# Single-row loads, small fp32 matmuls to spread them, row centring on GpSimd, and a new order of steps, in a linear-attention kernel with a feed-forward layer

## The chip, the cores and the metric

The kernel runs on one core of a Trainium2 chip. A core has five engines, each with its own in-order instruction stream: TensorE (PE; its weight loads are shown apart as PEld), VectorE (DVE), ScalarE (ACT), GpSimd (POOL) and SyncE (SP, which here only issues DMAs). Matmuls write to PSUM, the other operands lie in SBUF. Sixteen DMA engines move data between the memories; a DMA is issued from the queue of an engine, here mostly SyncE's. The metric is the device time of one execution in microseconds (us), lower is better.

## What is computed

A linear attention with decay (RWKV-like) over 4 batches, 8 heads, 768 steps and head size 48, then a layer norm, a feed-forward layer of 384 to 1536 to 384 with a ReLU, and a residual. Inputs and output are fp32.

```python
# r, k, v: (4, 8, 768, 48); w, u: (8, 48)
for t in range(S):
    kt, vt, rt = (k[:, :, t].copy(), v[:, :, t].copy(), r[:, :, t].copy())
    cur = np.einsum('bhd,bhe->bhde', u[None] * kt, vt)
    y[:, :, t] = np.einsum('bhd,bhde->bhe', rt, state + cur)
    state = w[None, :, :, None] * state + np.einsum('bhd,bhe->bhde', kt, vt)
...
# x: y with the heads side by side, (4, 768, 384)
mu = np.mean(x, axis=-1, keepdims=True)
var = np.mean((x - mu) ** 2, axis=-1, keepdims=True)
xn = (x - mu) / np.sqrt(var + 1e-06) * g_ln
ch = np.maximum(xn @ w_ch1, 0.0) @ w_ch2
return (x + ch).astype(np.float32)
```

## The kernel before

The sequence of each batch is cut into 6 chunks of 128 steps, 24 chunks in all. Inside a chunk the recurrence is written as matrix products: k is scaled by w to the power −(t+1) and r by w to the power t (the tables Fk and Fr), their product under a causal mask gives the scores, and a state Z carries what earlier chunks left. The tables come from log w: one copy of w spread over all 128 partitions (WB, L178), its logarithm (LN, L232), and two exponentials whose scale is a column of step numbers (FR at L238, FK at L235). The same w, and u, are also needed as columns, with the head dimension along the partitions: four small loads (ROWS, L186) bring them as 48 × 4 columns of two partition halves. From them come uwI (UW, the product u·w) and WLZ (WL, the power 128 of w, by which the state decays over a chunk). The scale g of the layer norm is spread over the partitions by a load (GB, L181).

For each chunk i the steps are, in the names of the code: LK, LR, LV load k, r, v (128 partitions × 8 heads × 48, 192 KB each, all from SyncE's queue); SK and SR scale k and r into the bf16 tile sc (L168, the helper `times`, on VectorE or GpSimd); CV casts v to vv; TR turns sc by eight TensorE transposes (L284), TC copies them out of PSUM to trs; for chunks from 9 on a transposing DMA (TD, L305) does it instead. AT makes the scores (L320), AM masks them (L330, VectorE), Q multiplies r and k columns (L168). S gives the diagonal term and the new state (L351, L364), CC copies the diagonal's factors, ZU and ZD form the state Z, VB multiplies v by the diagonal's factors (L383), Y sums up the output in PSUM (L393, L401), X adds the diagonal and row sums (L408, VectorE). Then SQ takes the squares on ScalarE, RS the reciprocal root on GpSimd, and XN centres the row and multiplies by g (L421 the mean, L422 one VectorE operation); the reciprocal root is applied only at the very end, since the ReLU lets a positive factor through. LT and XT (or the transposing DMA LTD) turn xn; UP is the up-projection (L458), RL the ReLU out of PSUM into hT (ScalarE L474 or VectorE L476), DN the down-projection (L486), OT scales and adds x (L542), STO stores. Chunks 8 to 19 go through the up-projection in pairs, the others alone (GROUPS). The last chunk's down-projection is done in two halves (DA, DB, L501; OA, OB, L517) so that the first can be stored while the second runs. Weights w1 and w2 come as three loads each from GpSimd's queue, cast to bf16 on the way (IW1, IW2).

TensorE has work only once chunks have been loaded, scaled and turned; until then steps named DU run matmuls on a tile of zeros (L227, L229), their size in columns written in the plan.

The order is written out by hand: PLAN is one list of steps, each with its number and the engine (v VectorE, s ScalarE, g GpSimd, − fixed). Every engine executes its share of the list in the list's order, and waits by semaphores for what its operands need; tiles rotate through small rings (SLOTS), and the PSUM tiles named tr, at, s, y and o exist once each.

## Time and profile before

| | us |
|---|---|
| median of 3 runs | 162.78 |
| lowest and highest run | 160.44, 163.22 |
| the profiled execution | 160.98 |
| its span, first to last instruction | 159.2 |

| engine | busy us | share of the span | instructions |
|---|---|---|---|
| TensorE matmuls | 143.0 | 90% | 1769 |
| VectorE | 132.3 | 83% | 265 |
| GpSimd | 88.3 | 55% | 119 |
| ScalarE | 69.4 | 44% | 155 |

The granted TensorE clock is 1.00 throughout. The queue of SyncE carries 98,560 packets, 23.8 MB, most of them of 192 bytes (one head's row of one step).

The page has, besides totals, the busy share of each engine in 40 equal slices; a view by stretch gives the same in microseconds between chosen times. The chain of waits follows the work that ended last back to what released it; "SPq L186" in it means that SyncE's queue was issuing the DMA of line 186, "DMA kf<-in_k_dram" that a load of k was in flight. A line of the timeline has the start, the duration, the engine, the line, the operation, output and inputs and, in brackets, how long the engine stood idle before and what released it. Durations of the helper lines (L163, L165, L168) belong to several steps, so they are told apart by their tiles.

### The profile page before, as it was taken

Reading aid. Unit: us, or ns where it says so; the run is one execution under the profiler, and the core shown is the slowest. Engines: PE = TensorE matmul, PEld = TensorE weight load, DVE = VectorE, ACT = ScalarE, POOL = GpSimd, SP = SyncE. Lnnn points to the kernel's source line nnn. Section 1 sums busy time; section 2 is a strip of 40 time slices with the busy share of each in tenths; the row PEclk is TensorE's granted clock in tenths of the full one; section 3 lists DMA queues with packets and bytes.
Section 4 is the critical chain, followed back from the end, with each engine's and each line's share of the span. In section 5 each row is a group of like instructions: output and inputs, shape, how many; then the busy total and the mean of one; then the engine's idle time right before and its main releaser. Section 6 shows DMA issues by size and latency. Waiting matters only on the chain.

```text
span 159.2 us, 4407 instructions
## 1 busy us (share of the span) xinstructions
PE 143.0 (90%) x1769; PEld 109.1 (69%) x1769; DVE 132.3 (83%) x265; ACT 69.4 (44%) x155; POOL 88.3 (55%) x119
## 2 busy tenths in 40 slices
PE   5896959499999989799999988997999999999991
PEld 2244737398877777677787757784787767888881
DVE  2457998696899999998889999999979999996132
ACT  3427644653821844646653644614184412700510
POOL 2332465899594665979769865559327420850100
PEclk9999999999999999999999999999999999999999
DMA  3899999999989959999999999895899772314212
GB/s 89 156 173 211 184 184 191 216 199 232 198 157 182 192 110 215 168 218 122 247 235 183 219 224 145 207 214 105 180 215 197 157 195 45 124 29 124 99 54 101
DMA packets 100356, 26.64 MB, mean 167 GB/s; under 512 B 95344, under 2 KB 99952, under 8 KB 100336
## 3 DMA queue, kind: packets, MB, share of 16 engines
q1 hardware_dynamic: 98560, 23.80, 75.0%
q0 software_dynamic: 1632, 2.36, 8.9%
q8 instruction: 14, 0.23, 0.6%
q10 hardware_dynamic: 144, 0.20, 0.5%
q14 instruction: 6, 0.05, 0.1%
HBM read 19.27 MB, written 4.72 MB: 151 GB/s over the span
## 4 chain that ended last, share of the span: by engine, by line
DVE 37%; PE 29%; SPq 10%; POOL 8%; issue 8%; DMA 6%; ACT 0%; DVEq 0%; POOLq 0%
PE hp L458 13%; PE o L486 12%; DVE A L330 8%; DVE xn L422 6%; DVE x L408 4%; SPq L265 4%; DVE Z L168 3%; DMA kf<-in_k_dram 3%; DVE ot L542 3%; DVE hT L476 3%; DVE ZS L377 3%; POOL sc L168 3%; DVE sc L168 3%; DMA trs<-sc 2%; SPq L262 2%
## 5 line engine op out<-in xcount | busy, mean ns | idle before, releaser
L458 PE MATMUL hp<-xT,w_sb 128*128 128x128 bf16 (+1 forms) x648 | 57.6, 238 | 0.6 <-DVE hT L476 0.6
L486 PE MATMUL o<-w_sb,hT 128*128 128x384 bf16 x276 | 53.3, 326 | 2.9 <-DVE ot L542 2.9
L458 PEld LDWEIGHTS <-w_sb 128*128 128x128 bf16 x648 | 48.7, 114 | 5.2 <-issue 0.7
L474 ACT ACTIVATE hT<-hp 128x512 bf16<-128x512 f32 x51 | 30.2, 596 | 44.9 <-PE hp L458 44.3
L486 PEld LDWEIGHTS <-hT 128*128 128x128 bf16 x276 | 25.2, 97 | 15.5 <-issue 3.4
L330 DVE TENSOR_TENSOR A<-at,mask 128x1024 bf16<-128x1024 f32 x24 | 29.1, 1215 | 1.8 <-PE at L320 1.8
L383 POOL TENSOR_TENSOR Vb<-vf,cc 128x384 f32<-128x384 f32 x14 | 12.3, 876 | 13.7 <-DVE cc L165 7.0
L422 DVE SCALAR_TENSOR_TENSOR xn<-x,mu,g_bc 128x384 bf16<-128x384 f32 x24 | 19.0, 792 | 0.8
L168 POOL TENSOR_TENSOR sc<-rf,Fr 128x384 bf16<-128x384 f32 x14 | 15.6, 1117 | 7.2 <-DMA rf<-in_r_dram 7.2
L542 DVE SCALAR_TENSOR_TENSOR ot<-o,rs,x 128x384 f32<-128x384 f32 x23 | 14.0, 610 | 5.8 <-PE o L486 5.7
L168 POOL TENSOR_TENSOR q<-trs 128x512 bf16<-128x512 bf16 x13 | 16.3, 1251 | 2.3 <-ACT trs L163 2.2
L428 POOL TENSOR_SCALAR rs<-sq 128x1 f32<-128x1 f32 (+1 forms) x18 | 3.9, 217 | 23.5 <-ACT sqj L415 22.5
L168 POOL TENSOR_TENSOR sc<-kf,Fk 128x384 bf16<-128x384 f32 x12 | 13.4, 1119 | 5.8 <-DMA kf<-in_k_dram 5.8
L476 DVE TENSOR_SCALAR hT<-hp 128x512 bf16<-128x512 f32 x21 | 14.3, 683 | 2.6 <-PE hp L458 2.6
L408 DVE SCALAR_TENSOR_TENSOR x<-y,Vb 128x384 f32<-128x384 f32 x24 | 13.2, 550 | 2.8 <-POOL Vb L383 2.1
L415 ACT ACTIVATE sqj<-x,sm 128x384 bf16<-128x384 f32 x24 | 14.7, 613 | 1.8 <-DVE cc L165 1.1
L227 PE MATMUL o<-warm 128*128 128x512 bf16 x45 | 13.3, 433 | 1.7 <-DVE u_p L194 1.7
L163 ACT COPY trs<-tr 128x1024 bf16<-128x1024 bf16 x8 | 8.1, 1011 | 12.5 <-PE tr L284 12.5
L168 DVE TENSOR_TENSOR sc<-kf,Fk 128x384 bf16<-128x384 f32 x12 | 9.0, 750 | 5.0 <-ACT Fk L235 4.5
L431 POOL TENSOR_TENSOR rs<-rs,expo 128x1 f32<-128x1 f32 (+1 forms) x18 | 12.0, 668 | 1.5
L320 PE MATMUL at<-trs 48*128 48x128 bf16 x192 | 9.6, 219 | 1.8 <-DVE A L330 1.7
L163 ACT CAST vv<-vf 128x384 bf16<-128x384 f32 x16 | 8.1, 513 | 4.5 <-DMA vf<-in_v_dram 4.5
(66 smaller groups left out, 169.8 us busy)
## 6 DMA issues: line engine op xcount, KB each, us to landing
kf<-in_k_dram SPq DMA_DIRECT2D x24, 192.0 KB, 4.3
rf<-in_r_dram SPq DMA_DIRECT2D x24, 192.0 KB, 4.4
vf<-in_v_dram SPq DMA_DIRECT2D x24, 192.0 KB, 4.2
out_dram<-ot SPq DMA_DIRECT2D x23, 192.0 KB, 2.3
w_sb<-in_moe_w_ch_dram POOLq DMA_DIRECT2D x6, 384.0 KB, 5.9
trs<-sc SPq DMA_TRANSPOSE x15, 3.6
w_bc<-in_w_dram ACTq DMA_DIRECT2D x1, 192.0 KB, 3.8
g_bc<-in_moe_g_ln_dram SPq DMA_DIRECT2D x1, 192.0 KB, 5.7
```

Source lines behind the costliest of these rows:

```text
L163: nc.scalar.copy(out=out, in_=in_)
L168: engines[e].tensor_tensor(out=out, in0=in0, in1=in1, op=ALU.mult)
L227: nc.tensor.matmul(out=warm_ps[0][:], lhsT=warm[:, :P], rhs=warm[:], start=True, stop=True)
L330: nc.vector.tensor_tensor(out=AA(i)[:, a:b].rearrange("p e q t -> p (e q) t"), in0=psum["at", i][:, a:b].rearrange("p e q t -> p (e q) t") ...
L408: nc.vector.scalar_tensor_tensor(out=xx(i)[:], in0=psum["y", i][:, :C], scalar=1.0, in1=Vb(i)[:], op0=ALU.mult, op1=ALU.add, accum_out=sm[ ...
L415: nc.scalar.activation(out=sqj[:], in_=xx(i)[:], func=ACT.Square, bias=sm[i][:], scale=-float(C), accum_out=sq[g][:, j : j + 1])
L422: nc.vector.scalar_tensor_tensor(out=xn(g)[:, j], in0=xx(i)[:], scalar=mu[i][:], in1=g_bc[:], op0=ALU.subtract, op1=ALU.mult,)
L458: nc.tensor.matmul(out=t[:, a * gw : (a + 1) * gw], lhsT=w1_sb[n][:, kc, fb::FB], rhs=xT(g)[:, :size, kc, :], start=(kc == 0), stop=(kc == ...
L474: nc.scalar.activation(out=o, in_=s, func=ACT.Relu)
L476: nc.vector.tensor_relu(out=o, in_=s)
L486: nc.tensor.matmul(out=psum["o", i][:, :C], lhsT=hT(g)[:, fk, j * P : (j + 1) * P], rhs=w2_sb[d][:, a, :], start=(fk == 0), stop=(fk == FK ...
L542: nc.vector.scalar_tensor_tensor(out=ot(i)[:], in0=psum["o", i][:, :C], scalar=rs[g][:, j : j + 1], in1=xx(i)[:], op0=ALU.mult, op1=ALU.add,)
```

## The change

- w, u and g are each loaded as one row of one partition: w from SyncE's queue (WF), u and g from ScalarE's (UF, GF). The spread loads WB and GB and the four column loads ROWS are gone.
- The logarithm is taken of the one row (LN). A matmul of a column of ones with it (fp32, 384 columns, WBM) spreads it over the partitions into PSUM, from where the two exponentials read. g is spread by a second such matmul (GBM) and copied to SBUF by VectorE (GB).
- The columns come from eight matmuls of one column each (fp32, WT): rows of log w and of u·w (UWR, GpSimd, on one row) are turned into PSUM; UW copies the one to uwI on VectorE, WL takes the exponential of the other for WLZ.
- XN can be given to GpSimd: then the mean, the subtraction and the product are three GpSimd operations. In the new plan chunks 1, 2, 8, 9, 13, 14, 16, 19 and 21 are.
- The memsets of sc (MP) can be given to GpSimd; three of six are.
- PLAN is replaced as a whole: the order of loads, of steps and the engines. By count: SR from 10 on VectorE and 14 on GpSimd to 14 and 10; Q from 11 and 13 to 9 and 15; VB from 10 and 14 to 11 and 13; ZD from 6 and 6 to 5 and 7; CC from 11 on VectorE and 13 on ScalarE to 16 and 8; CV from 2 on VectorE, 16 on ScalarE, 6 on GpSimd to 3, 13, 8; XT from 4 on VectorE and 12 on ScalarE to 6 and 10; RL from 21 and 51 to 22 and 50. Which chunks are turned by DMA, GROUPS, SLOTS and the sizes of all tiles stay. The zero matmuls (DU) go from 25,264 columns in 12 steps to 16,000 in 10.

```diff
 PLAN = """
-WB,0,s LK,0,- MP,2,v MI,0,g MP,1,v TL,0,s LR,4,- MP,5,v MP,3,v LR,0,- MW,0,v MP,0,v ROWS,3,- LN,0,s ROWS,1,- FR,0,s LR,1,- FK,0,s ROWS,2,- SK,0,v
-LK,2,- LK,1,- SR,0,v ROWS,0,- MZ,0,v LV,0,- DU,7984,- TR,0,- MP,4,v LR,2,- TC,0,s SR,4,g LV,1,- MM,0,g DU,2848,- AT,0,- LK,3,- Q,0,g AM,0,v LK,4,-
...
+MW,0,v GF,0,s LK,0,- MP,0,v MP,3,g MO,0,v MM,0,g UF,0,s WF,0,- MP,1,v MZ,0,v MI,0,g LK,1,- TL,0,s MP,4,v LK,2,- MP,2,g LR,0,- LN,0,s DU,2992,-
+WBM,0,- UWR,0,g LR,2,- LV,2,- GBM,0,- FR,0,s LV,0,- FK,0,s WT,0,- SK,2,g LR,1,- SR,2,v WL,0,s SK,0,g LV,1,- SR,0,v DU,896,- TR,2,- GB,0,v CV,2,s
+LR,4,- TC,2,v SK,1,v CV,0,g DU,1808,- TR,0,- LR,3,- UW,0,v AT,2,- Q,2,g TC,0,s SR,1,v LK,4,- AM,2,v CV,1,g DU,1920,- TR,1,- LK,3,- Q,0,g AT,0,-
...
+    xc = const.tile([P, C], FP32, name="xc")
...
-    def spread(t):
-        return bass.AP(tensor=t.tensor, offset=t.offset, ap=[[0, P], [1, C]])
...
+    def row(t):
+        return bass.AP(tensor=t.tensor, offset=t.offset, ap=[[C, 1], [1, C]])
+
+    def WF(i, e):
+        queues[e].dma_start(out=w_row[:].rearrange("p h d -> p (h d)"), in_=row(w))
...
     def LN(i, e):
-        nc.scalar.activation(out=ln_bc[:].rearrange("p h d -> p (h d)"), in_=w_bc[:], func=ACT.Ln)
+        nc.scalar.activation(out=ln_row[:, :, :D], in_=w_row[:], func=ACT.Ln)
+
+    def WBM(i, e):
+        t = psum["wb"] = ps.tile([P, 512], FP32, name="y")
+        nc.tensor.matmul(out=t[:, :C], lhsT=ones[:], rhs=ln_row[:, :, :D], start=True, stop=True)
+        psum["ln"] = t[:, :C].rearrange("p (h d) -> p h d", h=H)
...
+    def GBM(i, e):
+        t = psum["gb"] = ps.tile([P, 2, HP, P], FP32, name="at")
+        nc.tensor.matmul(
+            out=t[:, 0].rearrange("p q t -> p (q t)")[:, :C], lhsT=ones[:], rhs=g_row[:], start=True, stop=True
+        )
...
+    def UWR(i, e):
+        times("g", uw_row[:, :, :D], u_row[:], w_row[:])
+
+    def WT(i, e):
+        t = psum["wt"] = ps.tile([P, 512], FP32, name="s")
+        first = True
+        for a, src in enumerate((ln_row, uw_row)):
+            flat = src[:].rearrange("p (q e) d -> p q (e d)", e=2)
+            for q in range(HP):
+                nc.tensor.matmul(
+                    out=t[:, a * HP + q : a * HP + q + 1], lhsT=flat[:, q, :], rhs=ones[:, :1],
+                    start=first, stop=True, skip_group_check=True,
+                )
+                first = False
...
     def XN(i, e):
         g, j, _ = group_of[i]
-        nc.vector.tensor_scalar(out=mu[i][:], in0=sm[i][:], scalar1=1.0 / C, scalar2=None, op0=ALU.mult)
-        nc.vector.scalar_tensor_tensor(
-            out=xn(g)[:, j], in0=xx(i)[:], scalar=mu[i][:], in1=g_bc[:], op0=ALU.subtract, op1=ALU.mult,
-        )
+        engines[e].tensor_scalar(out=mu[i][:], in0=sm[i][:], scalar1=1.0 / C, scalar2=None, op0=ALU.mult)
+        if e == "v":
+            nc.vector.scalar_tensor_tensor(
+                out=xn(g)[:, j], in0=xx(i)[:], scalar=mu[i][:], in1=g_bc[:], op0=ALU.subtract, op1=ALU.mult,
+            )
+        else:
+            nc.gpsimd.tensor_scalar(out=xc[:], in0=xx(i)[:], scalar1=mu[i][:], scalar2=None, op0=ALU.subtract)
+            times(e, xn(g)[:, j], xc[:], g_bc[:])
```

The first steps of the new plan in TensorE's order: zeros of 2,992 columns, WBM, GBM, WT, zeros of 896, TR of chunk 2, zeros of 1,808, TR of chunk 0, AT of chunk 2, zeros of 1,920, TR of chunk 1, AT of chunk 0. The loads of k, r and v follow on SyncE's queue in the order k0, (w), k1, k2, r0, r2, v2, v0, r1, v1, r4, r3, k4, k3, k5, v3, r5. The first up-projection stands behind Y of chunk 2.

More of the change, by code (lines that the diff above doesn't have):

```diff
@@ L144 @@
     Fk = const.tile([P, H, D], FP32, name="Fk")
[L145 removed]
+    w_row = const.tile([1, H, D], FP32, name="w_row")
+    u_row = const.tile([1, H, D], FP32, name="u_row")
+    g_row = const.tile([1, C], FP32, name="g_row")
+    ones = const.tile([1, P], FP32, name="ones")
+    ln_row = const.tile([1, H, DP], FP32, name="ln_row")
+    uw_row = const.tile([1, H, DP], FP32, name="uw_row")
     g_bc = const.tile([P, C], FP32, name="g_bc")
[L147 to L150 removed]
     WLZ = const.tile([P, HP, E2], FP32, name="WLZ")
@@ L215, in MP @@
     def MP(i, e):
-        nc.vector.memset(sc(i)[:, :, :, D:DP], 0.0)
+        engines[e].memset(sc(i)[:, :, :, D:DP], 0.0)
     def MZ(i, e):
@@ L242, in UW @@
             p0 = par * DP
-            times("g", uwI[p0 : p0 + D, :, par], u_p[p0 : p0 + D, :], w_p[p0 : p0 + D, :])
+            nc.vector.tensor_copy(out=uwI[p0 : p0 + D, :, par], in_=psum["wt"][p0 : p0 + D, HP : 2 * HP])
     def WL(i, e):
-        nc.scalar.activation(out=ln_p[:], in_=w_p[:], func=ACT.Ln)
         for par in range(2):
```

113 lines of the change are left out of this document (52 added, 61 removed).

## The prediction

> **What bounds the kernel now.** I read the page's busy table and its 40 slices first, then the busy time by stretch, then the chain of waits in order of time, then single instructions of the start.
>
> The busy table and the slices: TensorE and VectorE are both near full from about 40 us to 120 us; in the first 28 us VectorE has holes, and TensorE's share there is mostly zeros, as shown below. The DMA row is full long before the engines are.
>
> ```profile
> PE 143.0 (90%) x1769; PEld 109.1 (69%) x1769; DVE 132.3 (83%) x265; ACT 69.4 (44%) x155; POOL 88.3 (55%) x119
> ...
> PE   5896959499999989799999988997999999999991
> DVE  2457998696899999998889999999979999996132
> ...
> DMA  3899999999989959999999999895899772314212
> ```
>
> The busy time by stretch (columns: length, then busy us and count of PE, PEld, DVE, ACT, POOL, then clock, DMA share, GB/s):
>
> ```profile
> 0.00:8.00 8.00, 5.49 (x16) 1.98 (x16) 2.69 (x10) 2.92 (x4) 2.33 (x11) 1.00 0.62 122
> 8.00:16.00 8.00, 6.54 (x64) 3.79 (x65) 5.09 (x13) 3.94 (x8) 2.34 (x4) 1.00 1.02 193
> 16.00:24.00 8.00, 6.25 (x95) 4.43 (x95) 7.77 (x14) 4.12 (x7) 4.65 (x5) 1.00 1.03 185
> 24.00:27.20 3.20, 3.13 (x43) 2.08 (x43) 3.16 (x8) 1.49 (x2) 1.45 (x3) 1.00 1.16 187
> 27.20:34.00 6.80, 4.52 (x85) 3.90 (x83) 4.86 (x13) 3.61 (x7) 6.23 (x7) 1.00 1.19 208
> 40.00:120.00 80.00, 75.69 (x958) 59.66 (x956) 75.61 (x149) 39.61 (x96) 54.41 (x65) 1.00 0.98 187
> ```
>
> The first up-projection matmul starts at 27.2 us. Of TensorE's 21.4 us busy until then, 16.3 us (rows L227 and L229 of the same view) are matmuls on zeros. From 27.2 us to TensorE's last end at 155.95 us it is busy 121.6 of 128.8 us. So the time is the start, then a stretch in which two engines are full together. VectorE is idle 11.7 us before 40 us, 4.4 of the 80 us after it.
>
> What sets the start is shown by the chain of waits: until 17 us it never leaves SyncE's queue.
>
> ```profile
> 1.85 2.62 SPq L265
> 4.47 0.04 issue
> 4.51 0.70 SPq L186
> 5.22 0.05 issue
> 5.27 0.44 SPq L186
> ...
> 14.95 0.81 SPq L268
> 15.76 0.04 issue
> 15.80 1.18 SPq L181
> 17.03 5.28 DMA kf<-in_k_dram
> ```
>
> L186 issues the four loads of u and w columns, L181 the spread of g: 0.70 + 0.44 + 0.58 + 1.12 + 1.18 = 4.02 us of issue in front of loads of k, r and v.
>
> **The parts.** *Loads.* The four column loads and the spread of g leave SyncE; one row of w joins it (0.45, its shortest issue of this kind): −3.6 us of queue. On the DMA engines the spread of w and of g go too. g landed 2.7 us after the load ahead of it (18.86 to 21.55); w lay ahead of or beside the first k. The sixteenth large load is r of chunk 5 in both orders. It lands at 23.05 now. With k 0 at 4.9 (now 5.29) and 1.04 us a load (ten landings from 8.49 to 18.86) it lands at 20.5, with 0.77 us (the first three steps) at 16.5: 2.5 to 6.5 us sooner. The rows of u and g go out on ScalarE's queue ahead of its table load, beside 1.2 us in which that engine was idle: nothing on the path.
>
> *Fk and Fr.* Today w lands at 4.54, the logarithm takes 0.52, Fr and Fk end at 5.8 and 6.3. After: the row is issued at 1.2 and lands 2.5 us later (the small loads' median) to 3.8 (the spread's), so at 4.4; logarithm 0.52; fp32 matmul with 384 columns, not in this trace, bounded by 0.33 (bf16, same columns) and four times that, taken near the top, 1.1, since it falls into the slow first matmuls (0.43 us for 512 columns until 5.9 us against 0.21 behind); then 0.61 + 0.60. Fk ends near 7.2, +0.9 us (0 to +1.5). It is on the path of the first scaled tiles, whose loads land at 6 to 8 us. The columns by one-wide matmuls, the two copies (0.06 to 0.2 each) and WLZ are wanted only at the first Z (13.65 now); the copy of g (0.35, as xT L165) lies on VectorE, and without cover costs itself.
>
> *First up-projection.* Its predecessor in TensorE's order is Y of chunk 2, which waits on X of chunk 1 for its bank. Ahead of that X, behind Fk, VectorE has seven scalings (0.56), three masks (1.215), two Z (0.545), two X with accumulator read (0.63), one xn with mean (0.94), two cc (0.16), trs 0.68, g 0.35, uwI 0.12: 3.9 + 3.65 + 1.1 + 1.3 + 0.9 + 0.3 + 1.15 = 12.3, so 19.5 us unhindered. Today's stretch from 6.3 to 27.2 holds 3.2 us of idle VectorE and some 1.9 us of scalings stretched by GpSimd (1.28 and 1.55 against 0.55). I add 3.5: 23.0 (21 to 25), 4.2 us earlier. The orders differ in what is done by then: seven chunks turned now, five after; one score product more and one state product fewer now: 2 × 0.61 + 0.40 − 0.57, about 1 us of real TensorE work falls behind the point. 3.2 us are left by TensorE's count.
>
> *VectorE in all*, by mean rows: xn and its mean −9 × (0.79 + 0.15) = −8.4; r scaled +4 × 0.67; q −2 × 0.45; cc +5 × 0.16; vv, hT, Vb one more each, 0.76 + 0.68 + 0.68; xT +2 × 0.35; Z −0.95; the rest about 0. Sum −4.0.
>
> *GpSimd.* Each moved xn is a mean (0.2), a subtraction not in this trace (0.5 to 1.1; 0.67 by the one-input cast vv L165, the nearest) and a product (1.12, as sc L168): 2.0 us for 0.94. Nine are +18; with r −4.5, q +2.5, vv +1.3, Z +1.1, the rest 0: +18, so 106 of some 155 us.
>
> That is not free for VectorE:
>
> ```profile
> 6.20 1.00 POOL L168 TENSOR_TENSOR sc<-rf,Fr 128x384 bf16<-128x384 f32 x1 [4.65 <-DMA rf<-in_r_dram]
> 6.33 1.28 DVE L168 TENSOR_TENSOR sc<-kf,Fk 128x384 bf16<-128x384 f32 x1 [4.49 <-ACT Fk L235]
> 7.54 0.64 DVE L168 TENSOR_TENSOR sc<-rf,Fr 128x384 bf16<-128x384 f32 x1
> ```
>
> The scaling beside GpSimd's takes 1.28, and 0.55 is the shortest of its kind. VectorE's operations with two inputs in SBUF show it, those out of PSUM do not (mask 1.21 to 1.23, always). Mean less shortest, times count: sc 3.7, xn 4.2, Z 2.4, Vb 1.3, q 0.4: 12 us over 73, 0.165 each. After there are 66. At GpSimd's share of 0.69 for 0.55 each pays 0.206: +2.7. VectorE's net is −1.3 (−4.0 if the stretch stays).
>
> The Trainium skill's "SBUF — State Buffer", section "Who interferes with whom", speaks against the change here: the pair of ports that VectorE and GpSimd share is an exclusive lock for a whole instruction, and the later comer is blocked. The trace agrees in kind: that scaling ends at 7.61, 0.41 us behind GpSimd's end at 7.20. By the rule the nine moved rows bring eighteen new holds; how many of VectorE's two-input operations meet one is the third rival.
>
> *TensorE.* The zero matmuls shrink from 25,264 to 16,000 columns; they lie in waits. Real work is the same but for the fp32 matmuls, whose wait is counted. The end keeps its two half tiles (0.42 each) and stores.
>
> **The sum.** By TensorE: 3.2 us. By VectorE: the idle before 40 us shrinks by the 4.2 less the later Fk, 3.3, plus 1.3 of work, 4.6. I take 3.8. The profiled execution took 160.98 (span 159.2, 1.8 around): 157.2. The median of the runs is 162.78, 1.8 above it; 159.0 on that scale. The result is again a median of few runs, which scattered by 2.8: I put it between, 158.1.
>
> **Rivals.** (1) *The sooner loads buy nothing*, since VectorE limits the start: 7.77 of 8 us busy at 16 to 24. Against it: 2.9 us idle at 8 to 16 and 3.2 behind 27.2. Then only 1.3 us come: 159.7 by the profiled execution, about 160.5 between the scales.
>
> (2) *TensorE's clock rises late.* The first block of zeros is 2,992 columns instead of 7,984, 2.5 us at the early rate, and then TensorE waits for the logarithm. Today the rate doubles 4.1 us after the first matmul. If it stays low until TR of chunk 1, 4,624 columns of zeros in front of real work take 3.9 instead of 1.9 us, +2: 160.1. For it: the gap; against: TensorE is not the start's limit.
> The Trainium skill's "TensorE: Matmul & The Clock Gate", "What's actually happening", wants about 3.4 us of sustained work for the full rate; 2.5 us would not do, and the result by it is this rival's.
>
> (3) *GpSimd takes back more than it gives.* Place: VectorE's two-input operations from 27 to 120 us. At today's price of 0.165 a piece the 4.0 hold 1.2 for seven operations fewer, so 2.8 are work at shortest times. If a piece costs twice as much, 0.33, on the way to the 0.40 that Z pays already (mean 0.95, shortest 0.55), the stretch is 66 × 0.33 = 21.8 for 12.0, and VectorE grows by 9.8 − 2.8 = 7.0 us; less the 3.3 of the start +3.7: 164.7, 165.6 between the scales. From 0.27 a piece ((12.0 + 2.8 + 3.3) / 66) it is slower than now. For it: GpSimd is already busy 54.4 of 80 us in the stretch where VectorE is the limit, and five of the nine rows (chunks 13 to 21) fall into it; against: the other four rows come early, four scalings of r leave GpSimd.
>
> (4) *The stretch stays as it is* and VectorE keeps the whole 4.0: 2.7 us more, 154.5 by the profiled execution, 155.4.
>
> **Chances.** Forecast 0.45, (1) 0.21, (2) 0.06, (3) 0.16, (4) 0.12. The forecast's own range is 156 to 160.5. To hold 8 in 10 the range takes in (1), (2) and half of (4) and the near end of (3): 154 to 164. The bound of 2% is 3.3 us, about what a measurement of this kernel can tell with runs scattering by 2.8; the forecast lies just beyond it, so 0.36 of its 0.45 count as faster, with all of (4) and 0.02 of (1): 0.50. Within: 0.09 + 0.19 + 0.06 = 0.34. Slower: (3), 0.16.
>
> **What would show it.** Right: SyncE's chain without L186 and L181 lines, Fk's end near 7.2, the first L-hp matmul near 23 us, VectorE over 0.9 busy from 12 us on, GpSimd at 104 to 108 us, VectorE at 130 to 132. Wrong: the first hp matmul behind 26 us (rival 1), L227 matmuls of 0.43 us behind 8 us (rival 2), the mean of sc or xn on VectorE above 0.9 us or Vb from GpSimd as the leading releaser (rival 3), VectorE under 129 us (rival 4).

## The result, and the profile after

| | before | after |
|---|---|---|
| median of the runs, us | 161.66 (4 runs, 160.44 to 163.22) | 169.62 (4 runs, 168.85 to 171.09) |
| the profiled execution, us | 160.98 | 169.34 |
| its span, us | 159.2 | 167.3 |

The changed kernel is slower: the ratio is 1.053, with a 95% interval of 1.039 to 1.067. The forecast was 158.1 us, faster. A ratio, here and below, leaves out executions that took over 1.5% longer than the fastest of the same kernel in their batch, so it is not exactly the quotient of the medians.

The busy table and the slices of the changed kernel, the same lines as were shown of before, and GpSimd's with them:

```profile
PE 147.5 (88%) x1763; PEld 111.9 (67%) x1766; DVE 133.4 (80%) x259; ACT 66.3 (40%) x143; POOL 113.4 (68%) x148
...
PE   6998788886999989889899889797999999799970
...
DVE  5058999997688999989998979979699989676350
...
POOL 5428969996095777999986995999987065670100
...
DMA  4999999999900999898379947969989796321221
```

In these rows VectorE is at 8 in the fourth slice (12.5 us) and at 9 from the fifth (16.7 us; the forecast was 12). But from the tenth on (38 us) it falls to 6 and 7 again and again, where before it stood at 8 and 9 nearly always, and GpSimd is at 9 in most of the slices from the 17th to the 29th. GpSimd has 25.1 us more work than before (113.4 against 88.3), where 18 were forecast. The DMA row has a hole of two slices at 46 to 54 us.

The busy time by stretch, in the columns shown before (length, busy us and count of PE, PEld, DVE, ACT, POOL, clock, DMA share, GB/s):

```profile
0.00:8.00 8.00, 6.58 (x17) 3.39 (x17) 2.19 (x10) 2.86 (x4) 3.84 (x15) 1.00 0.78 152
8.00:16.00 8.00, 7.51 (x58) 5.60 (x61) 5.95 (x9) 2.61 (x5) 4.66 (x5) 1.00 1.10 218
...
24.00:27.20 3.20, 2.34 (x30) 1.56 (x32) 3.20 (x9) 0.51 (x2) 2.24 (x4) 1.00 1.25 212
27.20:34.00 6.80, 6.01 (x112) 5.42 (x109) 6.50 (x12) 3.75 (x6) 6.38 (x8) 1.00 1.08 197
40.00:120.00 80.00, 73.56 (x922) 56.39 (x922) 70.29 (x134) 36.89 (x88) 63.94 (x78) 1.00 0.80 162
```

In the 80 us from 40 on VectorE is busy 70.29 us instead of 75.61, TensorE 73.56 instead of 75.69, GpSimd 63.94 instead of 54.41. So the loss there isn't work on the two engines that were full; they wait, while the third has more to do. (The clock column reads 1.00 in the first stretches too; that TensorE worked at half its rate there shows only in the lengths of its matmuls, see below.)

The chain of waits at the start, in order of time (start, length, what):

```profile
1.25 2.19 DMA w_row<-in_w_dram
...
3.52 0.53 ACT ln_row L232
...
4.10 1.64 PE y L236 x2
5.74 1.28 PE at L247 x2
7.02 3.20 PE s L263 x16
10.22 0.54 PE o L227
10.76 0.32 PE o L229
11.08 0.87 PE tr L312 x8
```

But for one issue of 0.46 us, SyncE's queue has left this part of the chain, as forecast. In its place stand 6.1 us of small fp32 matmuls: the spread of log w (L236), that of g (L247) and the sixteen pieces of the one-wide ones (L263). The first turn (L312) starts at 10.88. Before, it started at 8.23 and waited for nothing but its scaled tile:

```profile
8.23 0.62 PE L284 MATMUL tr<-ident,sc 128*128 128x128 bf16 x8 [1.00 <-DVE sc L168]
```

The shares of the chain by engine, of before and of the changed kernel, then by line of the changed one:

```profile
DVE 37%; PE 29%; SPq 10%; POOL 8%; issue 8%; DMA 6%; ACT 0%; DVEq 0%; POOLq 0%
...
POOL 33%; PE 25%; DVE 15%; DMA 14%; issue 6%; SPq 4%; ACT 0%; POOLq 0%; DVEq 0%; ACTq 0%
PE o L518 9%; PE hp L490 8%; POOL xc L455 7%; POOL q L170 6%; POOL sc L170 6%; POOL xn L170 5%; DMA w_sb<-in_moe_w_ch_dram 3%; DVE A L358 3%; DVE sc L170 3%; DMA vf<-in_v_dram 3%; POOL Vb L411 2%; DMA rf<-in_r_dram 2%; DMA xT<-xn 2%; POOL rs L463 2%; DMA kf<-in_k_dram 2%
```

VectorE had 37% of this chain and GpSimd 8%; now GpSimd has 33%, and its largest single line is xc, the subtraction that the change brought there. The groups of instructions (line, engine, operation, tiles and shapes, count, then busy us and mean ns of one, then the engine's idle time before it) give its price:

```profile
L455 POOL TENSOR_SCALAR xc<-x,mu 128x384 f32<-128x384 f32 x9 | 12.0, 1337 | 0.9
L170 POOL TENSOR_TENSOR xn<-xc,g_bc 128x384 bf16<-128x384 f32 x9 | 9.4, 1044 | 0.8
```

The row by which the prediction sized the subtraction is this one of the kernel before:

```profile
L165 POOL CAST vv<-vf 128x384 bf16<-128x384 f32 x6 | 4.0, 668 | 5.6 <-DMA vf<-in_v_dram 5.6
```

The subtraction, with one tensor read and a column of scalars, takes 1.34 us, twice the cast and more than the product of two tensors that follows it.

### The profile page after: what moved, and what is told of

Read it like the earlier page. It is cut to its first block, busy times and chain, and to the rows that moved or that the text cites. A ratio compares the mean times of both kernels' runs of the same rounds, so it can differ in the third digit from the quotient of the medians.

```text
span 167.3 us, 4404 instructions
## 1 busy us (share of the span) xinstructions
PE 147.5 (88%) x1763; PEld 111.9 (67%) x1766; DVE 133.4 (80%) x259; ACT 66.3 (40%) x143; POOL 113.4 (68%) x148
## 4 chain that ended last, share of the span: by engine, by line
POOL 33%; PE 25%; DVE 15%; DMA 14%; issue 6%; SPq 4%; ACT 0%; POOLq 0%; DVEq 0%; ACTq 0%
PE o L518 9%; PE hp L490 8%; POOL xc L455 7%; POOL q L170 6%; POOL sc L170 6%; POOL xn L170 5%; DMA w_sb<-in_moe_w_ch_dram 3%; DVE A L358 3%; DVE sc L170 3%; DMA vf<-in_v_dram 3%; POOL Vb L411 2%; DMA rf<-in_r_dram 2%; DMA xT<-xn 2%; POOL rs L463 2%; DMA kf<-in_k_dram 2%
## 5 line engine op out<-in xcount | busy, mean ns | idle before, releaser
L490 PE MATMUL hp<-xT,w_sb 128*128 128x128 bf16 (+1 forms) x648 | 57.0, 237 | 1.2 <-DVE xT L167 0.7
L506 ACT ACTIVATE hT<-hp 128x512 bf16<-128x512 f32 x50 | 29.4, 597 | 46.4 <-PE hp L490 46.2
L170 POOL TENSOR_TENSOR q<-trs 128x512 bf16<-128x512 bf16 x15 | 19.2, 1282 | 2.9 <-DVE trs L167 2.6
L443 ACT ACTIVATE sqj<-x,sm 128x384 bf16<-128x384 f32 x24 | 14.8, 615 | 5.4 <-DVE x L436 5.3
L170 DVE TENSOR_TENSOR sc<-rf,Fr 128x384 bf16<-128x384 f32 x14 | 10.8, 784 | 6.0 <-DMA rf<-in_r_dram 6.0
L451 DVE SCALAR_TENSOR_TENSOR xn<-x,mu,g_bc 128x384 bf16<-128x384 f32 x15 | 13.4, 893 | 0.5
L170 POOL TENSOR_TENSOR Z<-ZS,WLZ 128x384 bf16<-128x384 f32 x7 | 7.0, 1003 | 9.2 <-PE at L348 5.1
L455 POOL TENSOR_SCALAR xc<-x,mu 128x384 f32<-128x384 f32 x9 | 12.0, 1337 | 0.9
L463 POOL TENSOR_TENSOR rs<-rs,expo 128x1 f32<-128x1 f32 (+1 forms) x18 | 11.2, 625 | 1.5
L460 POOL TENSOR_SCALAR rs<-sq 128x1 f32<-128x1 f32 (+1 forms) x18 | 5.2, 289 | 10.1 <-ACT sqj L443 8.8
L170 POOL TENSOR_TENSOR sc<-rf,Fr 128x384 bf16<-128x384 f32 x10 | 10.7, 1070 | 0.0
```

Source lines behind the costliest of these rows:

```text
L170: engines[e].tensor_tensor(out=out, in0=in0, in1=in1, op=ALU.mult)
L443: nc.scalar.activation(out=sqj[:], in_=xx(i)[:], func=ACT.Square, bias=sm[i][:], scale=-float(C), accum_out=sq[g][:, j : j + 1])
L451: nc.vector.scalar_tensor_tensor(out=xn(g)[:, j], in0=xx(i)[:], scalar=mu[i][:], in1=g_bc[:], op0=ALU.subtract, op1=ALU.mult,)
L455: nc.gpsimd.tensor_scalar(out=xc[:], in0=xx(i)[:], scalar1=mu[i][:], scalar2=None, op0=ALU.subtract)
L463: nc.gpsimd.tensor_tensor(out=rs[g][:], in0=rs[g][:], in1=expo[:, :n], op=ALU.pow)
L490: nc.tensor.matmul(out=t[:, a * gw : (a + 1) * gw], lhsT=w1_sb[n][:, kc, fb::FB], rhs=xT(g)[:, :size, kc, :], start=(kc == 0), stop=(kc == ...
```

## The experiments

Ratios are against the kernel before, run on the same chip in turn; the interval is 95%. The batches of runs lay on different chips, on which the median of the kernel before was 160.05 to 162.89 us. So what an edit is worth is read from the ratios and not from the medians; a point is 1%, some 1.6 us.

### Did the loads bound the start?

The first two runs take the kernel before and free SyncE's queue, nothing else. The one drops the column loads and the spread of g (the columns of w and u stay constants and g is 1, so the output lacks them); the other issues them from ScalarE's queue, behind FK.

```diff
 # no_columns
-ROWS,3,- ROWS,1,- ROWS,2,- ROWS,0,- GB,0,-
 # columns_on_scalar
-ROWS,3,- ROWS,1,- ROWS,2,- ROWS,0,- GB,0,-
+ROWS,3,s ROWS,1,s ROWS,2,s ROWS,0,s GB,0,s
```

> The kernel before without the four column loads and without the spread of g: the columns are the constants 1 and 0, g is set to 1 by VectorE, so decay, bonus and scale of the norm are left out of what is computed. It bounds what freeing SyncE and the DMA engines of them can be worth. If those 4 us of issue were on the path: 157.5 to 160 us against some 162. If not: 161 to 163.

> The kernel before with its four column loads and the spread of g issued from ScalarE's queue, behind the exponential for Fk, instead of SyncE's; nothing else moves. It tests the first step of the prediction alone: 4 us of issue in front of loads. If those slots were on the path: 157.5 to 160 us against 161.9, first up-projection at 24 to 25.5 us. If the loads are held by the DMA engines and not by the issue: 161 to 162.5.

Measured: 0.9963 (0.991 to 1.0016) and 0.9973 (0.9923 to 1.0023), so no change in either. In no_columns the r of chunk 5 lands at 18.95 us instead of 23.05, but the first up-projection comes at 29.0 us, not sooner than the 27.2 of before; in columns_on_scalar it comes at 31.8, where 24 to 25.5 had been expected if the issues were on the path. The busy time by stretch of no_columns:

```profile
8.00:16.00 8.00, 7.22 (x78) 4.29 (x77) 6.11 (x14) 4.06 (x9) 2.33 (x4) 1.00 1.10 218
16.00:24.00 8.00, 5.49 (x81) 3.76 (x79) 7.77 (x12) 4.11 (x7) 7.51 (x7) 1.00 1.20 211
24.00:28.00 4.00, 3.73 (x27) 2.04 (x29) 3.96 (x10) 0.93 (x2) 2.15 (x3) 0.58 1.04 187
```

VectorE is as full at 16 to 24 us as before (7.77 of 8), TensorE waits more there (5.49 instead of 6.25), and then its granted clock has a mean of 0.58 over 4 us. By the lower end of the interval, 0.991, the freed queue is worth 1.4 us at most in this order, and that it is worth anything isn't shown. Rival 1 had given it nothing. The two executions of no_columns in which the clock stayed at 1.00 took 158.2 and 158.5 us, its other ones 159.3 to 160.8; but two executions of before, at a mean clock of 0.99, took 158.3 and 158.8 as well.

Two more take the changed kernel and move single issues ahead of what they waited behind. After the issue at 36.06 SyncE's queue stood until 52.7, because the transposing DMA of chunk 10 waited in it for a scaling on VectorE (15.0 us); and the loads of the second weight are issued by GpSimd behind two centred rows, and landed 2.6 to 3.9 us later than before.

```diff
 # loads_first
+LK,11,- LV,9,- LR,12,-
 TD,10,-
 ...
-LK,11,-
 ...
-LV,9,-
 ...
-LR,12,-
 # weights_early
+IW2,0,g
 XN,1,g
 ...
+IW2,1,g
 XN,2,g
+IW2,2,g
```

> The changed kernel with k 11, v 9 and r 12 issued ahead of the transposing DMA of chunk 10 instead of behind it. Theory Q: 164 to 167, the DMA engines no longer empty from 42 to 52 us. Theory G: 169 to 170, the loads were not wanted that early. Theory S: 169 to 170.

> The changed kernel with the three loads of w2 issued from GpSimd's queue ahead of and between the first two moved rows (chunks 1 and 2) instead of behind them and three more steps. If the late landing of w2 (40.5 to 45.5 us, in the kernel before 36.6 to 42.8) costs what TensorE and VectorE wait at 39 to 46 us: 166 to 168. If it is cover for something else that is late: 169 to 170.

Measured: 1.0429 (1.0362 to 1.0497) and 1.0502 (1.0441 to 1.0564), inside the interval of the changed kernel. So neither the hole in the loads nor the late weights is shown to cost time; the 164 to 167 us and 166 to 168 us by which they would have been the cause were missed.

### The order, the engines and the rows, taken apart

Seven kernels mix the two plans. The first gives the nine rows back to VectorE in the new order; the second gives them alone to GpSimd in the old order; the third and fourth exchange the engines of the steps that both plans have (in new_engines with the nine rows); the last three join starts and rests of the two plans, or put the single-row loads and the fp32 matmuls into the old order, with 5,840 columns of zeros fewer at its start. Chunk 1's row stands ahead of the first up-projection in the new plan; so new_start_old_rest keeps that one row on GpSimd, against what its expectation says, and old_start_new_rest has eight.

```diff
 # xn_vector (after, nine rows)
-XN,1,g
+XN,1,v
 # rows_on_gpsimd (before, the same nine rows)
-XN,1,v
+XN,1,g
 # old_engines (after, order kept)
-SK,2,g SK,0,g TC,2,v CV,0,g
+SK,2,v SK,0,v TC,2,s CV,0,s
 # new_engines (before, order kept)
-SR,4,g CV,0,s SK,2,v CC,0,s XN,1,v
+SR,4,v CV,0,g SK,2,g CC,0,v XN,1,g
 # new_start_old_rest (after until the first up-projection, then before's list)
-UP,2,- X,2,v DU,336,- AT,4,- RL,2,v
+LR,6,- LK,6,- LV,5,- SR,6,v LV,6,-
 # old_order_rows (before's list, new setup)
-DU,2848,-
+WT,0,- GBM,0,- GB,0,v
```

> The changed kernel with its nine GpSimd rows of XN given back to VectorE, all else and the order as changed. Theory G (GpSimd takes back more than it gives: subtraction and product take 1.34 + 1.05 us where 0.67 + 1.12 were reckoned, and hold the in-order queue): 160 to 164 us against the 169.6 of the changed kernel, GpSimd near 90 us busy, VectorE near 140. Theory Q (SyncE's queue: a transposing DMA that waits 15 us stands ahead of loads): 167 to 170, since the queue still stands. Theory S (the start, TensorE held by fp32 matmuls): 168 to 172, VectorE's 8 us more coming on top.

> The kernel before with the nine XN alone (chunks 1, 2, 8, 9, 13, 14, 16, 19, 21) on GpSimd: VectorE gets rid of some 8.4 us, GpSimd gets 24 (0.3 + 1.34 + 1.05 each). If GpSimd's queue and the shared port give it back with more: 165 to 169 us. If VectorE's relief is worth what was reckoned: 158 to 161.

> The changed kernel's order, but every step that the two plans share (other than the setup and the loads of weights) on the engine that it had before; 129 steps move back, the nine XN among them. Theory E (the choice of engines is the loss: VectorE is busy 139.6 us with the nine rows given back, 7 us over the kernel before, for r scaled, cc, xT and others that came to it): 162 to 165 us, VectorE near 134 us busy. Theory O (the order is the loss, whatever the engines): 168 to 172.

> The order and the loads of the kernel before, but the shared steps on the engines of the changed kernel, nine XN on GpSimd among them. Theory E: 168 to 172 us. Theory O: 162 to 165.

> The changed kernel up to its first up-projection, then all steps that are left in the order and on the engines of the kernel before (no XN on GpSimd but none is in the first part either). In the changed kernel's trace the first up-projection starts at 27.3 us, in the kernel before at 27.2. Theory R (the loss is in the order of the rest): 160 to 163 us, as the kernel before. Theory S (the start leaves something behind that costs later): 166 to 170.

> The kernel before up to its first up-projection, with its loads, then all steps that are left in the order and on the engines of the changed kernel, the nine rows on GpSimd among them. Theory R: 166 to 170. Theory S: 160 to 164.

> The order of steps of the kernel before with only the loads changed: single rows, logarithm of one row, spreading and turning by fp32 matmuls; all XN on VectorE. If the loads by themselves are worth what was predicted for the start: 157 to 159 against some 161.7 of the kernel before. Theory S (the fp32 matmuls cost 6 us of TensorE between the logarithm and the first turn, so that the first scaled chunk waits): 161 to 164, first up-projection no earlier than 27 us.

| kernel | median us | ratio (interval) |
|---|---|---|
| xn_vector | 168.83 | 1.0426 (1.037 to 1.0481) |
| rows_on_gpsimd | 176.02 | 1.1006 (1.0926 to 1.1087) |
| old_engines | 178.97 | not formed (176.27 to 180.32 us) |
| new_engines | 176.01 | 1.1004 (1.091 to 1.1098) |
| new_start_old_rest | 165.34 | 1.0156 (1.0063 to 1.025) |
| old_start_new_rest | 173.42 | 1.0651 (1.0566 to 1.0737) |
| old_order_rows | 166.99 | 1.0226 (1.0131 to 1.0321) |

The nine rows alone cost 16 us in the old order, about twice the loss that had been expected at most, and all the other exchanged engines add nothing to it (1.1004 beside 1.1006). VectorE's work fell in rows_on_gpsimd by 6.8 us (125.5 of 132.3), and still the kernel became slower. The view of one tile tells how; its last lines list who waited for it (us, times):

```profile
L428 POOL TENSOR_SCALAR xc<-x,mu x9: 1260/1263/1795, 29.0 to 144.4; 128x384 f32<-128x384 f32 x9
...
  PEld L448: 9.4, 4
  PE tr L448: 8.9, 4
```

That is the list of rows_on_gpsimd (L448 is the turn of the centred row): four times TensorE waited for a row from GpSimd, 9.4 us in all, and whatever stands behind that turn in its order waited too. The weight loads' waits for GpSimd, summed over tiles, are 14.0 us there (xn 9.4, q 4.6) and 2.3 before (q alone). The waiting can have a second price, seen in the stretches of the same run:

```profile
64.00:72.00 8.00, 5.55 (x85) 4.36 (x84) 6.89 (x10) 4.25 (x11) 7.58 (x10) 1.00 0.71 147
72.00:76.00 4.00, 1.08 (x14) 0.84 (x12) 1.02 (x2) 0.65 (x2) 3.73 (x5) 0.60 1.06 234
76.00:82.00 6.00, 6.00 (x51) 3.99 (x50) 3.00 (x6) 1.99 (x5) 4.37 (x6) 0.70 1.02 216
```

GpSimd is busy nearly throughout (3.73 of 4 us) while TensorE is busy for 1.08 of the 4 us from 72 to 76, and then TensorE, wholly busy again, has a mean granted clock of 0.70 over 6 us. Four of the runs above, rows_on_gpsimd, new_engines, new_start_old_rest and old_start_new_rest, had a mean clock of 0.95 to 0.98 in nearly every execution; so their ratios hold both prices, and the 16 us are not GpSimd's instructions alone.

xn_vector says that in the new order, which was made around those rows, giving them back gains about 1 point of the ratio at most, and its interval meets that of the changed kernel: the order leaves TensorE no wait for xn then, but VectorE has 139.6 us of work instead of 133.4. Neither half of the plan is good with the other's engines: old_engines took 176 to 180 us, beyond both of its expectations.

The joined plans put most of the loss behind the first up-projection (6.5 points with the new rest, 1.6 with the new start), with the lowered clock in both. old_order_rows, whose rows are all on VectorE, loses 2.3 points by the new loads and setup alone, where 157 to 159 us had been expected if the loads were worth what was predicted. In its trace the one-wide matmuls and the spread of g follow the first turn, from 9.73 to 14.8 us, and the first attention product comes at 15.44 us, where it came at 9.98 before.

What in the rows costs the time is not told by these seven.

### The setup's matmuls

low_setup is the changed kernel with bf16 copies of log w, u·w and g as operands of the small matmuls (the last digits of the three are lost).

```diff
-    ones = const.tile([1, P], FP32, name="ones")
-    ln_row = const.tile([1, H, DP], FP32, name="ln_row")
-    uw_row = const.tile([1, H, DP], FP32, name="uw_row")
+    ones = const.tile([1, P], BF16, name="ones")
+    ln_row = const.tile([1, H, DP], BF16, name="ln_row")
+    uw_row = const.tile([1, H, DP], BF16, name="uw_row")
...
+        nc.vector.tensor_copy(out=g_low[:], in_=g_row[:])
```

> The changed kernel with log w, u times w, the ones and g rounded to bf16 for the small matmuls, so that each runs in one pass; what is spread and turned loses digits, so the output is not the reference's. In the changed kernel's trace these matmuls hold TensorE from 4.1 to 10.2 us, 16 records of some 0.22 us for the columns and 0.8 us a pass for the spreads. If they hold back the start (theory S): first up-projection 2 to 4 us earlier than 27.3 and 166 to 168 us. If VectorE or the loads do: 169 to 170.

Measured: 166.38 us, 1.022 (1.0132 to 1.0307). The timeline of TensorE in the changed kernel, then in this one (start, length, engine, line, tiles, count):

```profile
4.10 1.64 PE L236 MATMUL y<-ln_row,ones 1*128 1x384 f32 x2 [0.25 <-ACT ln_row L232]
5.54 1.48 PE L247 MATMUL at<-g_row,ones 1*128 1x384 f32 x2
6.82 1.70 PE L263 MATMUL s<-ones,ln_row 1*128 1x1 f32 x8
8.38 1.84 PE L263 MATMUL s<-ones,uw_row 1*128 1x1 f32 x8
...
10.88 1.06 PE L312 MATMUL tr<-ident,sc 128*128 128x128 bf16 x8
```

```profile
4.26 0.47 PE L237 MATMUL y<-ln_row,ones 1*128 1x384 bf16 x1 [0.41 <-ACT ln_row L233]
4.53 0.52 PE L249 MATMUL at<-g_low,ones 1*128 1x384 bf16 x1
4.85 0.28 PE L265 MATMUL s<-ones,ln_row 1*128 1x1 bf16 x4
5.00 0.24 PE L265 MATMUL s<-ones,uw_row 1*128 1x1 bf16 x4
...
8.51 1.04 PE L314 MATMUL tr<-ident,sc 128*128 128x128 bf16 x8 [2.41 <-DVE sc L171]
```

An fp32 matmul appears as two instructions (x2, x8 for four). The spread takes 1.64 us instead of 0.47, the eight one-wide ones some 3.4 instead of 0.4. In bf16 all are over by 5.2 us, and the turn waits for its operand. The first up-projection comes at 25.7 us, 1.6 us earlier than in the changed kernel, a little less than expected. By the ratios the edit is worth 3.1 points, some 5 us, with an uncertainty of about 1.7 points from the two intervals; where it gains more than those 1.6 us is not shown. The Trainium skill's "FP8 and Floating Point Precision", section "TensorE Precision Notes", gives true FP32 four passes through the array; the 1.64 to 0.47, 3.5 times, agrees roughly. The one-wide ones, 3.4 to 0.4, cost more than four times as much.

### GpSimd's queue

no_subtract leaves mean and subtraction of the nine rows out (they are multiplied by g without being centred); scalar_centre computes the same as the changed kernel, with the subtraction on ScalarE.

```diff
 # no_subtract
-            nc.gpsimd.tensor_scalar(out=xc[:], in0=xx(i)[:], scalar1=mu[i][:], scalar2=None, op0=ALU.subtract)
-            times(e, xn(g)[:, j], xc[:], g_bc[:])
+            times(e, xn(g)[:, j], xx(i)[:], g_bc[:])
 # scalar_centre (mu with the factor -1/C)
-            nc.gpsimd.tensor_scalar(out=xc[:], in0=xx(i)[:], scalar1=mu[i][:], scalar2=None, op0=ALU.subtract)
+            nc.scalar.activation(out=xc[:], in_=xx(i)[:], func=ACT.Identity, bias=mu[i][:], scale=1.0)
```

> The changed kernel, but the nine rows on GpSimd are not centred: the mean and the subtraction are left out and only the product with g is made, so GpSimd has 9 x (1.34 + 0.25) = 14 us less to do. Theory P (what costs time behind the start is GpSimd's in-order queue, and in it the subtraction that I had put at 0.67 and that takes 1.34): VectorE's waits for Vb, rs, q and sc shrink and the time falls by 3 to 5 us, to 165 to 166.5, a ratio of 1.02 to 1.03. Rival (the order itself, whatever GpSimd has to do): by less than 1 us, a ratio of 1.042 or more.

> The changed kernel, with the subtraction of the nine rows on ScalarE (a copy with the negative mean as its bias) and mean and product left on GpSimd: GpSimd has 9 x 1.34 = 12 us less, ScalarE about 9 x 0.5 = 4.5 us more (its copies of this shape in the profile), and each row crosses between the engines twice. Theory P (GpSimd's queue): 166 to 167.5, 2 to 3 us faster than the changed kernel, a ratio of 1.025 to 1.035. Rival (the order itself): no change or slower, 1.045 or more, as ScalarE's own queue holds the row back.

Measured: 162.84 us, 1.0187 (1.0098 to 1.0275), and 164.07 us, 1.0235 (1.0166 to 1.0303). Both stand clear of the changed kernel's interval (1.0389 to 1.0671): moving one operation of nine rows gives 2.9 points, 4.7 us of 160.4. Both went a little beyond the range that the theory of GpSimd's queue gave. The first up-projection comes at 26.7 and 27.5 us, against 27.35, so most of the gain lies behind it: in the 80 us from 40 on TensorE is busy 75.83 and 76.33 us instead of 73.56. The page and a tile view of scalar_centre:

```profile
PE 148.8 (92%) x1766; PEld 112.1 (69%) x1766; DVE 131.0 (81%) x259; ACT 71.0 (44%) x152; POOL 103.1 (64%) x139
...
PE 46%; DVE 23%; POOL 12%; issue 6%; DMA 6%; ACT 2%; SPq 1%; POOLq 0%; DVEq 0%; ACTq 0%
```

```profile
L457 ACT ACTIVATE xc<-x,mu x9: 606/615/618, 26.7 to 135.7; 128x384 f32<-128x384 f32 x9
L170 POOL TENSOR_TENSOR xn<-xc,g_bc x9: 997/1002/1019, 27.4 to 136.4; 128x384 bf16<-128x384 f32 x9
```

ScalarE makes the subtraction in 0.62 us, GpSimd's work falls to 103.1 us, and its share of the chain from 33% to 12%, although each row crosses between the engines twice and GpSimd stood idle 6.8 us for it. TensorE's weight loads waited for GpSimd 6.1 us in the changed kernel (q 3.0, xn 2.6, sc 0.5), 2.4 in scalar_centre (0.9, 0.8, 0.7) and 1.1 in no_subtract (0.4 for q, 0.7 for sc). The 15.0 us wait of the transposing DMA became 6.7 in scalar_centre, which fits the same lateness. A rival is that GpSimd with less to do disturbs VectorE less: in scalar_centre VectorE's work fell by 2.4 us (131.0 of 133.4), and what that gave isn't told apart. In no_subtract it fell by only 0.9 (132.5), with the larger gain, so relief of VectorE isn't the main cause.

### Do the two prices add up?

Three kernels join two of the edits above, and one keeps fp32 but moves the one-wide matmuls: behind the first attention product, with the copies that read them, and without the zeros that followed them.

```diff
 # low_scalar_centre: low_setup and scalar_centre
 # low_xn_vector: low_setup and xn_vector
 # low_setup_old_rest: low_setup and new_start_old_rest
 # late_scalar_centre: scalar_centre and
-WT,0,- SK,2,g ... WL,0,s ... DU,896,- ... DU,1808,- ... UW,0,v AT,2,- ... TC,0,s ... AM,2,v
+SK,2,g ... AT,2,- WT,0,- ... TC,0,s WL,0,s ... AM,2,v UW,0,v
```

> The changed kernel with the subtraction of the nine rows on ScalarE and the setup's small matmuls reading bf16 copies (the last digits of log w, U and g are lost). Against the kernel before, the changed one stands at 1.053, the first edit alone at 1.0235 (2.9 points, 4.7 us of 160.4) and the second alone at 1.022 (3.1 points). Theory S (two prices in two stretches, the setup's matmuls before the first turn and the subtraction in GpSimd's queue behind it): they add up, 1.053 - 0.029 - 0.031 = 0.993, 159.3 us where the kernel before has 160.4, and the range 0.985 to 1.003. Rival (either edit takes away one and the same delay, as low_setup_old_rest at 1.026 suggests): not below 1.015.

> The changed kernel with the small matmuls in bf16 and the nine centred rows back on VectorE, in the new order. Alone the first gave 3.2 us and the second 0.8. Theory B (GpSimd's late rows and VectorE's extra work of 7 us are worth the same, wherever the start lies): 165.6, a ratio of 1.015 to 1.03. Rival (the slow setup hid what giving the rows back is worth, since VectorE waited for TensorE in the start): 163 or less, a ratio below 1.01.

> The changed kernel with two parts undone together: the small matmuls of the setup read bf16 copies (the last digits of log w, U and g are lost), and behind the first up-projection the steps stand in the order and on the engines of before. Each alone gave back time: the first 3.2 us (169.62 to 166.38), the second 4.3 us (165.34), against 7.7 us of loss beside the kernel before. Theory S (two separate prices, one of the setup on TensorE and one of the order and the engines behind it): they add up, 169.6 - 3.2 - 4.3 = 162.1, a ratio of 0.99 to 1.005. Rival (the two stand for one and the same delay, which either of them takes away): no lower than the better of the two, 165, a ratio of 1.012 or more.

> The changed kernel with the subtraction of the nine rows on ScalarE and all matmuls in fp32, but the sixteen one-wide ones that turn the columns stand behind the first attention product, with the copies that read them behind it too, and the zeros that followed them are gone: the first turn then follows the spread of g on TensorE, at about 8.5 us, not 10.64. Theory S2 (what the fp32 matmuls cost is their place in front of the first turn, 3.5 us of one-wide ones, not their number): the first turn comes 2 us sooner and the whole by about the 3.2 us that bf16 gave, a ratio of 0.99 to 1.01 beside 1.0235 for the subtraction alone. Rival (in the later place they stand in front of other work that is as urgent, since TensorE has no gap of 3.5 us there, or the slope of the first chunks hangs on loads): 1.02 or more, no gain.

| kernel | median us | ratio (interval) |
|---|---|---|
| low_scalar_centre | 162.40 | 1.0079 (1.0033 to 1.0125) |
| low_xn_vector | 164.87 | 1.0297 (1.0222 to 1.0371) |
| low_setup_old_rest | 164.32 | 1.0259 (1.0177 to 1.0341) |
| late_scalar_centre | 169.07 | 1.0517 (1.0418 to 1.0617) |

low_scalar_centre lies between the two expectations. The two edits gave 2.9 and 3.1 points each alone and 4.5 together, of 5.3. Together they gave more than either alone, clear of the intervals, so they are two prices; whether the 1.5 points that are missing from the sum are a delay that either edit takes away can't be said, since the four intervals together are wider than that. It is the fastest of the kernels with the new order, and 0.8% slower than the kernel before, so none of the versions beats that.

late_scalar_centre fell: the first turn came at 9.45 instead of 10.64 us, but the one-wide matmuls then ran from 12.73 to 16.30 us, right behind the first attention product, and the next zeros, turn and first state followed them.

```profile
11.24 1.01 PE L312 MATMUL tr<-ident,sc 128*128 128x128 bf16 x8 [0.78 <-DVE trs L167]
12.19 0.61 PE L348 MATMUL at<-trs 48*128 48x128 bf16 x8
12.73 1.86 PE L263 MATMUL s<-ones,ln_row 1*128 1x1 f32 x8
14.46 1.84 PE L263 MATMUL s<-ones,uw_row 1*128 1x1 f32 x8
16.63 1.06 PE L227 MATMUL o<-warm 128*128 128x512 bf16 x2 [0.33 <-issue]
17.48 0.53 PE L229 MATMUL o<-warm 128*128 128x384 bf16 x1
17.80 1.06 PE L312 MATMUL tr<-ident,sc 128*128 128x128 bf16 x8
```

VectorE also stood 2.8 us in front of the copy for uwI, with everything behind it in its order. The first up-projection came at 30.7 us, where scalar_centre has it at 27.5. At this place, too, TensorE had no 3.6 us free; another place wasn't tried.

low_setup_old_rest is no cheaper than new_start_old_rest, which speaks against adding up in this mixture. The first up-projection comes at 33.3 us in the one and at 33.0 in the other, so the quicker setup was lost before it. In the two stretches from 24 to 40 us the granted clock had a mean of 0.78 and 0.80 in the one, where TensorE was busy 2.20 of the first 8 us, and of 0.87 and 0.70 in the other; so both hold a loss by the clock, and the price of the setup can't be read from the pair. low_xn_vector lies above low_setup alone, whose interval it meets: giving the rows back gains nothing.

## Why the prediction was wrong

*The queue and the first up-projection* (step "Loads", and the 4.2 us of "First up-projection"). The loads came sooner as forecast: r of chunk 5 is issued by 14.83 instead of 18.14, and its neighbours in the queue land at 16.67 and 20.39. The first up-projection stayed, 27.35 against 27.2 (forecast 23.0, 21 to 25). That is rival 1's test, "behind 26 us". Two parts make up the 4.35 us, 1.9 and 2.4. The count of VectorE work behind Fk up to X of chunk 1 left out that VectorE's masks and all that follows them wait for the first turn, which came at 10.88 us instead of 8.23 (it also has two Z where the plan has three). That X, behind which the forecast put the up-projection at 23.0, ended at 24.94 us; in low_setup, with the first turn at 8.51, it ended at 23.34. And the up-projection doesn't follow that X at once. In TensorE's order the turn of chunk 4 stands in front of Y of chunk 2, and it waits for r of chunk 4, which VectorE scales behind that X:

```profile
25.28 1.65 DVE L170 TENSOR_TENSOR sc<-rf,Fr 128x384 bf16<-128x384 f32 x2
...
26.52 0.62 PE L312 MATMUL tr<-ident,sc 128*128 128x128 bf16 x8 [0.50 <-DVE sc L170]
...
27.35 0.84 PE L490 MATMUL hp<-xT,w_sb 128*128 128x128 bf16 x12
```

That is 2.4 us from the X to the up-projection, and 2.4 in low_setup too (23.34 to 25.74). The prediction had taken Y of chunk 2, and with it the X, for the last wait.

The premise behind this step, that the whole time moves with the first up-projection, failed as well. In the profiled execution of columns_on_scalar it came 4.5 us later than before (31.8 us), and that kernel takes the same time as the one before; rows_on_gpsimd has it at 27.0 and is 10% slower. And no_columns shows that the sooner loads were worth at most 1.4 us by themselves, in the old order.

*The columns* (step "Fk and Fr"). Fk ended at 6.89 us (forecast 7.2), so that part held. The one-wide matmuls were put at nothing because they are "wanted only at the first Z". Their results are; but on TensorE they stand ahead of the first turn, and TensorE executes its steps in order. They took 3.4 us there and the spread of g 1.3 more. The error is that it was asked who needs the result, not what stands behind the instruction. Price of both: 3.1 points of the ratio by low_setup, some 5 us.

*TensorE's rate* (rival 2). Its test came true: matmuls on 512 columns of zeros still took 0.43 us until 13.0 us, where before the rate had doubled by 6. Its price of 2 us wasn't measured alone. low_setup still has the low rate at 10.6 us, so a sooner full rate is no part of what it gained; but no run has the fp32 matmuls at the full rate, so whether they would cost less there is open. The Trainium skill's "TensorE: Matmul & The Clock Gate", "What's actually happening", wants about 3.4 us of sustained work. From 1.18 to 13 us the trace shows TensorE busy almost without a gap, 6.1 us of it with one-row fp32 matmuls, and still the low rate: by the Trainium skill's rule those don't count, or the rule isn't the whole of it. No run here tells which.

*GpSimd* (step "GpSimd"). The subtraction was taken at 0.67 us (0.5 to 1.1) by the cast; it took 1.34, outside the range, 6 us more in nine rows, and GpSimd had 113.4 us instead of 106 (test: 104 to 108). The Trainium skill's "GPSIMD Engine Reference", section "4.1 Engine selection", calls operations with one input on GpSimd roughly line-rate and those with two some twice as slow as on VectorE; here the one with one tensor input is the slower, 1.34 against 1.04, and the measurement decides. The larger error is that the sum had no term for this engine's lateness at all. It weighed GpSimd only by what it does to VectorE's operations, in the forecast and in rival 3 alike, while q, xn and sc are what TensorE's turns and products wait for. Rival 3 has the right side, but with 164.7 to 165.6 us less than half of the loss, and by a mechanism that didn't occur. Price of the subtraction in that queue: 2.9 points by scalar_centre, 4.7 us.

*VectorE* (step "VectorE in all" and rivals 3 and 4). Mean less shortest over the 66 two-input operations is 13.5 us, 0.205 each: the forecast was 0.206, so neither rival held (the mean of xn is 0.893, just under rival 3's 0.9). The kind of interference that the Trainium skill's "SBUF — State Buffer", section "Who interferes with whom", describes was there, at the forecast size. VectorE's 133.4 us lie above 130 to 132 in part for terms left out: memsets of the new rows (0.17 + 0.48 + 0.48), and the vv at a mean of 0.97 instead of 0.76.

So the side of the forecast was lost by two terms of the sum: some 5 us of TensorE's small matmuls put at nothing, and some 5 us of GpSimd's queue that had no term; undone together they give back 4.5 points, some 7 us. The gain of 3.8 us didn't come, since freeing SyncE's queue gave at most 1.4 us and the first up-projection hung on other work. low_scalar_centre, without the two prices, stands at 1.008 (1.003 to 1.013), with the first up-projection at 25.6: no gain is left that they hid. What makes the last 0.8% stays open. The late rate of TensorE is a candidate that wasn't tried: between 9.64 and 14.11 us, 3.1 us of zero matmuls, most of them at 0.43 us for 512 columns, stand in the chain of waits of low_scalar_centre.

## What to carry to other kernels

A step that is wanted late still costs its time if it stands early on an in-order engine: ask what is behind it there, and price it by the row in the same data type. An event at the start, such as the first up-projection, is no measure of the whole: check in a run whether the end moves with it. When work moves to a less busy engine, its share of busy time says little; look for which results of that engine the full ones wait for, and count how much later each comes. Where one operation in such a chain is slow, a third engine that does it in half the time can be worth two more crossings.

## What was unexpected in the hardware

- GpSimd's subtraction of a column (128 × 384, fp32 to fp32) takes 1.26 us at the shortest and 1.34 in the mean, longer than its product of two tensors with a bf16 output (1.00 to 1.04); ScalarE takes 0.62 for it.
- One-wide fp32 matmuls follow each other at 0.21 us for each of their two instructions, 3.4 us for eight matmuls, half of the 0.43 us of 512 bf16 columns in the same stretch; eight one-wide bf16 ones take 0.39 us together (4.85 to 5.24 us in low_setup).
- The granted clock falls in a program that runs on one core alone: to a mean of 0.58 over 4 us behind 8 us in which TensorE was busy 5.49 (no_columns), and of 0.60 and 0.70 over the 4 and 6 us from 72 us on in rows_on_gpsimd, where TensorE had stood still for 2.9 us. So waiting can cost twice. What releases the fall isn't shown: in the kernel before, TensorE was busy 4.52 of 6.8 us from 27.2 on, and the clock stayed at 1.00.
- DMAs issued from ScalarE's queue held its next copy back: in columns_on_scalar the first copy of turned columns began at 10.73 us instead of 8.89, after 4.38 us of idle time that a column load ended.
